# Two weight subtractions moved from VectorE to GpSimd, and the last row tile scaled by two engines

## The chip, the core and the metric

The kernel runs on one core of a Trainium2 chip. The metric is the device time of one execution in microseconds; lower is better. The core's engines run side by side, each through its own queue in order, and wait for one another through semaphores: TensorE (PE, with PEld for its weight loads), VectorE (DVE), ScalarE (ACT), GpSimd (POOL) and SyncE (SP, which issues most DMAs). GpSimd computes too, and it issues the DMAs that gather and scatter rows by a list.

## What is computed

Three layers follow each other, cut here to what matters:

```python
# 1: attention over keys and values averaged in groups of 8
scores = scale * q @ k_pooled.T;  attn = softmax(scores);  x = attn @ v_pooled   # -> 4608 x 512
# 2: a dense layer, 512 -> 2048 -> 512, with ELU between
x = elu(x @ w_in) @ w_out
# 3: a mixture of 8 experts, 512 -> 1024 -> 512, one expert per token
logits = x @ w_gate;  expert_idx = argmax(logits, axis=1);  gate_w = softmax(logits)[.., expert_idx]
for e in range(E):
    xe = x[expert_idx == e]
    h = np.maximum(xe @ w1[e], 0.0)
    out[expert_idx == e] = gate_w[expert_idx == e, None] * (h @ w2[e])
```

Everything is float32. The kernel multiplies at reduced precision with a correction: an operand is split into a high part (a cast to fp32r) and a low part (the operand minus its high part), and high x high, low x high and high x low are added up in PSUM.

## The kernel before

The change lies in the last stage, the experts. Tokens are sorted into lists by expert, and the lists are cut into tiles that the code runs one after the other: eight D tiles of 512 tokens, one S tile of 256 tokens (`S0`) and three T tiles of 128 tokens; three small U tiles of at most 32 tokens run beside others. The order of the tiles is D0 to D6, T0, D7, T1, S0, T2. So `main[-1]` is T2, a tile of one row group of 128 tokens, and S0 is the second to last.

A tile has four **units** (`i` = 0 to 3), each with 256 columns of the expert's hidden layer. For each unit:

- `m_load` issues two loads of 512 KB on SP, the first layer's weights (`w1st`, in T tiles `t1`) and the second layer's (`w2st`);
- `m_split` makes their high parts (`m1h`, `m2h`) with a ScalarE cast and their low parts (`m1l`, `m2l`) with a subtraction, by `split` at lines 129 to 131. Its parameter `eng` names the engine of the second layer's subtraction; without it that is VectorE. T tiles split the second layer alone;
- `m_g1` multiplies the tokens (`zh`, `zl`) with the first layer into `mh`; `m_act` applies the ReLU on ScalarE (`hh`) and makes the low part on VectorE (`hl`); `m_g2` multiplies `hh` and `hl` with the second layer and adds up into `my`, in the order `hh` x `m2h`, `hh` x `m2l`, `hl` x `m2h`.

`m_out` scales a finished tile's rows by the gate into `o`, ScalarE for even row groups and VectorE for odd ones, and `scatter` writes them to the output with an indirect DMA issued by GpSimd.

The order on each engine is the order in which the code is written, under a manual schedule. The function `mix(n)` writes step n: the first layer of unit n, the second layer of unit n - 1, the activations, the output of a tile that ended. Then `ahead(n)` lets loads and splits run ahead of their use, as far as a pool of 32 equal pieces of memory (`w_tile`) and reach limits allow. Freed pieces go to a queue and are given out again in turn, so a new tile can lie in the space of an older one; whoever writes it first waits for the older one's last reader. Around the change this gives: in the step where T1 starts, S0's units 1 and 2 are split; in the next, S0's unit 3; between them the low part of T1's own activations (`hlT`) is made on VectorE.

Of the kernel before, what the change touches and what calls it, by code (L numbers as in the profile page):

```python
# [20 lines left out]
B, H, S, D = 8, 8, 576, 64  # L21
POOLW = 8
SP = S // POOLW
DM = H * D
# [74 lines left out]
def fused_kernel(ctx: ExitStack, tc: tile.TileContext, q, k, v, w_in, w_out, w_gate, w1, w2, cst, out):  # L99
    nc = tc.nc  # L100
# [28 lines left out]
    def split(hi, lo, src, eng=None):  # L129
        nc.scalar.copy(hi, src)  # L130
        (eng or nc.vector).tensor_sub(lo, src, hi)
# [13 lines left out]
    def ring(pool, shape, dtype, tag, bufs, name):  # L145
        k = turns[tag] = (turns.get(tag, -1) + 1) % bufs
        return pool.tile(shape, dtype, tag=f"{tag}{k}", bufs=1, name=name)
# [19 lines left out]
    def w_tile(shape, dtype, name):  # L167
        slot_w[name] = k = free_w.pop(0)
        return wpool.tile(shape, dtype, tag=f"W{k}", bufs=1, name=name)

    def w_free(*names):
        for name in names:
            free_w.append(slot_w.pop(name))
# [904 lines left out]
    rows, sidxs, zs, wts, raws2, acts, yps, gates = {}, {}, {}, {}, {}, {}, {}, {}  # L1078
# [147 lines left out]
    def m_split(it, i, eng=None):  # L1226
        kind, s = it
        st, st2 = raws2.pop((it, i))
        if kind != "T":
            first = [w_tile([P, KC, 2 * P], F32R, f"m1{x}{kind}{s}_{i}") for x in "hl"]  # L1230
            split(*first, st)
        else:
            first = [st]
        second = [w_tile([P, 2, DM], F32R, f"m2{x}{kind}{s}_{i}") for x in "hl"]
        split(*second, st2, eng)
        wts[it].append((first, second))
        for name in (f"w1st{kind}{s}_{i}", f"w2st{kind}{s}_{i}"):
            if name in slot_w:
                w_free(name)
            if name in slot_s:  # L1240
                free_s.append(slot_s.pop(name))
# [65 lines left out]
    def m_out(it, i):  # L1307
        kind, s = it
        nu = TILES[kind]
        if i == 3:  # L1310
            for u in range(nu):
                o = ring(pools[1], [P, DM], F32, "o", 4, f"o{kind}{s}_{u}")
                gate = gates[it][:, u:u + 1]
                if u % 2 == 0:
                    nc.scalar.mul(o, yps[it][u], gate)
                else:
                    nc.vector.tensor_scalar_mul(o, yps[it][u], gate)
                scatter(out[:, :], o, sidxs[it][0][:, u:u + 1], NTOK)

    def scatter(dst, src, idx, n):  # L1320
        put = nc.gpsimd.indirect_dma_start(
            out=dst,
            out_offset=bass.IndirectOffsetOnAxis(ap=idx, axis=0),
            in_=src,
            in_offset=None,
            bounds_check=n - 1,
            oob_is_err=False,
        )
        tc.declare_no_dep(put.ins, group="out", reason="each token's row is written once")
        tc.add_to_no_dep_group("out", put.ins)  # L1330
# [53 lines left out]
    main = [("D", s) for s in range(KD)]  # L1384
# [45 lines left out]
    def ahead(n):  # L1430
        done = False
        while not done:
            done = True
            for what, reach, src in (("load", LOAD_REACH, units), ("split", SPLIT_REACH, split_units)):
                x = todo[what]
                if x == len(src):
                    continue
                need, it, i = src[x]
                if what == "split" and (need, it, i) not in units[:todo["load"]]:
                    continue  # L1440
                if need - when[n] > reach:
                    continue
                slots = SLOTS[it[0]][what == "split"]
                raw = STAGES[it[0]]
                if what == "load":
                    slots += max(0, raw - len(free_s))
                    if need - when[n] > 6 and raw > len(free_s) and len(free_w) < 12:
                        continue
                if slots > len(free_w):
                    continue  # L1450
                if what == "load":
                    m_load(it, i)
                else:
                    m_split(it, i)
                todo[what] += 1
                done = False

# [12 lines left out]
    for k in range(TURN_FROM, len(main)):  # L1470
        it, far = main[k], main[k - 1][0] == "T"
# [47 lines left out]
    def mix(n):  # L1519
# [11 lines left out]
        if n:  # L1531
            m_out(main[k0], i0)
# [3 lines left out]
        if n in casts_first:  # L1536
            for _, it2, half in todo_now:
                m_room(it2, half)
            ahead(n)
        elif k in side and i == 3:  # L1540
            u_out(side[k])
# [31 lines left out]
    with tc.manual_schedule(engines=ENGINES):  # L1573
        ahead(0)
        for n in range(8):
            mix(n)
        lpool["p"] = pools[1]
        for n in range(8, len(seq)):
            mix(n)
            if n == len(seq) - 6:  # L1580
                nc.gpsimd.drain()
        k0, i0 = seq[-1]
        m_g2(main[k0], i0)
        m_out(main[k0], i0)
# [85 lines left out]
```

## Time and profile before

| | |
|---|---|
| median of 3 runs | 1354.22 us (1353.72 to 1355.11) |
| the profiled execution | 1353.46 us, of it the span 1351.6 us |
| PE busy | 1336.7 us, 99% of the span |
| DVE busy | 1024.4 us, 76% |
| ACT busy | 798.8 us, 59% |
| POOL busy | 205.0 us, 15% |
| mean granted TensorE clock | 0.996 |
| S0's unit 1 split to the last scatter | about 1297 to 1347 us of the span |

The span is what the profiler saw of one execution; 1.9 us lie around it. A busy share is an average over the whole span. What a change at one place is worth is read from the engines' timelines at that place, by which wait ends last. In a row of a timeline a bracket gives the idle time of the engine just before the instruction and what ended it; a row without one followed at once.

### The profile page before, as it was taken

What the parts mean: (1) busy time and instruction counts of PE and PEld (TensorE: products, weight loads), DVE (VectorE), ACT (ScalarE), POOL (GpSimd) and SP (SyncE); (2) the same over time, 40 slices, a digit from 0 to 9 for tenths busy, and PEclk for the clock granted to TensorE, in tenths of its full rate; (3) what the DMA queues carried; (4) which work ended last, traced back from release to release, by engine and by line L of the source; (5) the groups of instructions that cost most, each with busy time, mean ns of one, the idle gap of its engine ahead of it and who ended that gap; (6) DMA issues with size and microseconds to landing.
All of it is one profiled execution on the core that took longest, in us unless ns stands there. A gap on an engine that the chain in (4) does not pass through costs nothing.

```text
span 1351.6 us, 23742 instructions
## 1 busy us (share of the span) xinstructions
PE 1336.7 (99%) x8398; PEld 1152.7 (85%) x8398; DVE 1024.4 (76%) x2479; ACT 798.8 (59%) x1949; POOL 205.0 (15%) x208
## 2 busy tenths in 40 slices
PE   9999999999999999999999999999999999999998
PEld 5799888888888889898988888988888888788787
DVE  7899888998888879797878787886646766646471
ACT  6777766676667676666666665562333444536261
POOL 0011011101211211111210000020213131212020
PEclk9999999999999999999999999999999999999999
DMA  9257443647354463555472432465576357768470
GB/s 349 71 175 213 126 100 83 84 78 80 74 80 70 83 69 63 86 66 82 73 94 48 64 40 47 90 161 117 164 119 186 125 179 257 267 200 299 156 275 23
DMA packets 109145, 169.43 MB, mean 125 GB/s; under 512 B 15509, under 2 KB 53015, under 8 KB 109016
## 3 DMA queue, kind: packets, MB, share of 16 engines
q1 hardware_dynamic: 91528, 135.45, 40.7%
q0 software_dynamic: 17488, 32.37, 12.5%
q8 instruction: 68, 1.11, 0.4%
q14 instruction: 61, 0.50, 0.2%
HBM read 146.35 MB, written 21.88 MB: 124 GB/s over the span
## 4 chain that ended last, share of the span: by engine, by line
PE 80%; DVE 8%; issue 5%; ACT 4%; DMA 2%; POOL 0%; SPq 0%; POOLq 0%; DVEq 0%; ACTq 0%
PE h L507 25%; PE y L549 25%; PE mhD L1261 12%; PE myD L1298 12%; PE pv L480 3%; PE sp L411 1%; DVE dec L228 1%; DVE dec L232 1%; DMA w2stD<-in_moe_w_dram 1%; DVE junk L600 1%; ACT gh L531 1%; ACT dec L221 1%; PE vsum L346 1%; DVE dec L226 1%; DVE g L524 1%
## 5 line engine op out<-in xcount | busy, mean ns | idle before, releaser
L549 PE MATMUL y<-woh,gh 128*128 128x512 f32 x576 | 229.8, 399 | 0.9 <-DVE yr L563 0.5
L549 PE MATMUL y<-woh,gl 128*128 128x512 f32 x576 | 226.4, 393 | 0.0
L549 PE MATMUL y<-wol,gh 128*128 128x512 f32 x576 | 226.2, 393 | 0.0
L600 DVE SCALAR_TENSOR_TENSOR junk<-yr,wgb 128x512 bf16<-128x512 f32 x264 | 180.9, 685 | 4.7 <-ACT yr L565 1.2
L531 ACT CAST gh<-g 128x384 fp32r<-128x384 f32 x192 | 98.5, 513 | 131.0 <-DVE g L525 111.9
L507 PE MATMUL h<-xh,wih 128*128 128x384 f32 x768 | 167.8, 340 | 2.3 <-ACT xh L493 1.5
L507 PE MATMUL h<-xl,wih 128*128 128x384 f32 x768 | 165.8, 337 | 0.0
L507 PE MATMUL h<-xh,wil 128*128 128x384 f32 x768 | 165.6, 337 | 0.0
L524 DVE SCALAR_TENSOR_TENSOR g<-g,th 128x384 f32<-128x384 f32 x192 | 106.3, 554 | 73.3 <-ACT th L519 72.7
L507 PEld LDWEIGHTS h<-xh,wih 128*128 128x128 f32 x768 | 138.3, 188 | 19.4 <-DVE g L525 2.1
L517 ACT ACTIVATE th<-h 128x384 f32<-128x384 f32 x192 | 94.1, 490 | 84.8 <-PE h L507 84.1
L1275 ACT ACTIVATE hhD<-mhD 128x512 fp32r<-128x512 f32 x64 | 38.3, 598 | 179.0 <-PE myD L1298 168.8
L507 PEld LDWEIGHTS h<-xh,wil 128*128 128x128 f32 x768 | 137.1, 188 | 0.0
L507 PEld LDWEIGHTS h<-xl,wih 128*128 128x128 f32 x768 | 136.9, 188 | 0.2
L1276 DVE SCALAR_TENSOR_TENSOR hlD<-mhD,hhD 128x512 fp32r<-128x512 f32 x64 | 44.2, 690 | 122.5 <-ACT hhD L1275 122.5
L549 PEld LDWEIGHTS y<-woh,gl 128*128 128x128 f32 x576 | 108.2, 188 | 23.6
L549 PEld LDWEIGHTS y<-woh,gh 128*128 128x128 f32 x576 | 108.1, 188 | 21.4 <-issue 1.0
L549 PEld LDWEIGHTS y<-wol,gh 128*128 128x128 f32 x576 | 108.2, 188 | 16.7
L532 DVE TENSOR_TENSOR gl<-g,gh 128x384 fp32r<-128x384 f32 x192 | 106.9, 557 | 19.9 <-ACT gh L531 17.0
L525 DVE TENSOR_TENSOR g<-g,h 128x384 f32<-128x384 f32 x192 | 106.3, 554 | 6.6
L519 ACT ACTIVATE th<-th 128x384 f32<-128x384 f32 x192 | 100.9, 525 | 6.1
L518 ACT ACTIVATE g<-th 128x384 f32<-128x384 f32 x192 | 100.9, 525 | 6.1
(287 smaller groups left out, 2387.2 us busy)
## 6 DMA issues: line engine op xcount, KB each, us to landing
wgb<-in_moe_w_gate_dram SPq DMA_DIRECT2D x96, 256.0 KB
w1stD<-in_moe_w_dram SPq DMA_DIRECT2D x32, 512.0 KB
w2stD<-in_moe_w_dram SPq DMA_DIRECT2D x32, 512.0 KB
qT<-in_q_dram SPq DMA_DIRECT2D x36, 256.0 KB
ybuf<-yr SPq DMA_DIRECT2D x33, 256.5 KB
raw<-in_moe_w_in_dram SPq DMA_DIRECT2D x16, 512.0 KB
raw<-in_moe_w_out_dram SPq DMA_DIRECT2D x15, 512.0 KB
t1U<-in_moe_w_dram SPq DMA_DIRECT2D x12, 512.0 KB
```

Source lines behind the costliest of these rows:

```text
L507: mark["g1"] = nc.tensor.matmul(ps, wi[i][a][:, c, o:o + P], bb[blk][:, c, :], start=n == 0, stop=n == 3 * KC - 1).ins
L517: nc.scalar.activation(th, hps[blk, f], AF.Relu, scale=-1.0)
L518: nc.scalar.activation(g, th, AF.Exp, scale=-1.0)
L519: nc.scalar.activation(th, th, AF.Tanh, scale=-0.5)
L524: nc.vector.scalar_tensor_tensor(g, g, 1.0, th, op0=ALU.add, op1=ALU.mult)
L525: nc.vector.tensor_max(g, g, hps.pop((blk, f)))
L531: nc.scalar.copy(gh, g)
L532: nc.vector.tensor_sub(gl, g, gh)
L549: nc.tensor.matmul(ys[blk][j], a[:, js], wo[i][bb][:, o, :], start=n == 0 and f in FIRST[blk], stop=n == 2 and f in LAST[blk],)
L600: nc.vector.scalar_tensor_tensor(junk, yrows[blk][j][:, :DM], 1.0, pes[blk, e], op0=ALU.mult, op1=ALU.mult, accum_out=lgs[blk][:, j, e:e + 1])
L1261: mark["g1"] = nc.tensor.matmul(ps[:, x], a[:, c, o * P:(o + 1) * P], y[:, c], start=k == 0, stop=k == len(terms) - 1).ins
L1298: nc.tensor.matmul(yps[it][u], a[:, us], second[w][:, o], start=i == 0 and o == 0 and n == 0, stop=i == 3 and o == 1 and n == 2,)
```

## The change

Two edits. In `ahead`, `m_split` gets GpSimd as its engine for units 1 and 2 of S tiles; of these tiles only S0 runs, so two subtractions of 128x1024 change the engine. In `m_out`, the last tile's row group is cut into two halves of 256 columns, the first scaled by ScalarE and the second by VectorE; the scatter behind them is the same.

```diff
             for u in range(nu):
                 o = ring(pools[1], [P, DM], F32, "o", 4, f"o{kind}{s}_{u}")
                 gate = gates[it][:, u:u + 1]
-                if u % 2 == 0:
+                if it == main[-1]:
+                    half = DM // 2
+                    nc.scalar.mul(o[:, :half], yps[it][u][:, :half], gate)
+                    nc.vector.tensor_scalar_mul(o[:, half:], yps[it][u][:, half:], gate)
+                elif u % 2 == 0:
                     nc.scalar.mul(o, yps[it][u], gate)
...
                 if what == "load":
                     m_load(it, i)
                 else:
-                    m_split(it, i)
+                    m_split(it, i, nc.gpsimd if it[0] == "S" and i in (1, 2) else None)
```

The order shows what this does to the queues. Numbers in names are tile and unit: `m2lS0_1` is the low part of the second layer's weights of S0's unit 1, `oD7_3` the fourth row group of D7's output. In brackets stand the semaphores for which a row waits, by the engine or the DMA queue that counts them. GpSimd's queue at the end of D7, before:

```order
L1321 DMA out_0_dram<-oD7_0_14501,oidxD7_12701 4608x512 [waits DMAHW5_49,DMASW0_49,Activation_49]
L1321 DMA out_0_dram<-oD7_1_14506,oidxD7_12701 4608x512 [waits DMASW1_49,DVE_49]
L1321 DMA out_0_dram<-oD7_2_14511,oidxD7_12701 4608x512 [waits DMASW2_49,Activation_49]
L1321 DMA out_0_dram<-oD7_3_14516,oidxD7_12701 4608x512 [waits DMASW3_49,DVE_49]
L1321 DMA out_0_dram<-oT1_0_14675,oidxT1_13152 4608x512 [waits DMAHW2_49,DMASW4_49,Activation_49]
```

and now:

```order
L1325 DMA out_0_dram<-oD7_0_14501,oidxD7_12701 4608x512 [waits DMAHW5_49,DMASW0_49,Activation_49]
L1325 DMA out_0_dram<-oD7_1_14506,oidxD7_12701 4608x512 [waits DMASW1_49,DVE_49]
L1325 DMA out_0_dram<-oD7_2_14511,oidxD7_12701 4608x512 [waits DMASW2_49,Activation_49]
L1325 DMA out_0_dram<-oD7_3_14516,oidxD7_12701 4608x512 [waits DMASW3_49,DVE_49]
L131 ISA
L131 TENSOR_TENSOR m2lS0_1_14530<-w2stS0_1_14421,m2hS0_1_14529 128x1024 [waits DMAHW6_49,DMAHW2_49,Activation_49]
L131 TENSOR_TENSOR m2lS0_2_14551<-w2stS0_2_14429,m2hS0_2_14550 128x1024 [waits DMAHW1_49,DMAHW0_49,DMAHW5_49,PE_49,Activation_49]
L1325 DMA out_0_dram<-oT1_0_14675,oidxT1_13152 4608x512 [waits DMASW4_49,Activation_49]
```

The two subtractions stand between D7's last scatter and T1's, and an `ISA` row came in ahead of them; the built program names this instruction a reload of a library, with index 0. VectorE's queue at the same place, before:

```order
L131 TENSOR_TENSOR m1lS0_1_14526<-w1stS0_1_14419,m1hS0_1_14525 128x1024 [waits DMAHW5_49,Activation_49]
L131 TENSOR_TENSOR m2lS0_1_14530<-w2stS0_1_14421,m2hS0_1_14529 128x1024 [waits DMAHW6_49,Activation_49]
L131 TENSOR_TENSOR m1lS0_2_14547<-w1stS0_2_14427,m1hS0_2_14546 128x1024 [waits DMAHW7_49,Activation_49]
L131 TENSOR_TENSOR m2lS0_2_14551<-w2stS0_2_14429,m2hS0_2_14550 128x1024 [waits DMAHW0_49,Activation_49]
L1276 SCALAR_TENSOR_TENSOR hlT1_1_0_14575<-mhT1_1_0_14558,hhT1_1_0_14574 128x256 [waits DVE_49,Activation_49]
L131 TENSOR_TENSOR m1lS0_3_14579<-w1stS0_3_14521,m1hS0_3_14578 128x1024 [waits DMAHW1_49,Activation_49]
L131 TENSOR_TENSOR m2lS0_3_14583<-w2stS0_3_14523,m2hS0_3_14582 128x1024 [waits DMAHW2_49,DVE_49,Activation_49]
L1175 TENSOR_TENSOR zlS0_14600<-zmS0_0_14418,zhS0_14599 128x4x256 [waits Activation_49]
L1276 SCALAR_TENSOR_TENSOR hlT1_2_0_14610<-mhT1_2_0_14590,hhT1_2_0_14609 128x256 [waits Activation_49]
```

and now:

```order
L131 TENSOR_TENSOR m1lS0_1_14526<-w1stS0_1_14419,m1hS0_1_14525 128x1024 [waits DMAHW5_49,Activation_49]
L131 TENSOR_TENSOR m1lS0_2_14547<-w1stS0_2_14427,m1hS0_2_14546 128x1024 [waits DMAHW7_49,Activation_49]
L1276 SCALAR_TENSOR_TENSOR hlT1_1_0_14575<-mhT1_1_0_14558,hhT1_1_0_14574 128x256 [waits DVE_49,Activation_49]
L131 TENSOR_TENSOR m1lS0_3_14579<-w1stS0_3_14521,m1hS0_3_14578 128x1024 [waits DMAHW1_49,Activation_49]
L131 TENSOR_TENSOR m2lS0_3_14583<-w2stS0_3_14523,m2hS0_3_14582 128x1024 [waits DMAHW2_49,DMAHW6_49,Activation_49,Pool_49]
L1175 TENSOR_TENSOR zlS0_14600<-zmS0_0_14418,zhS0_14599 128x4x256 [waits DVE_49,Activation_49]
L1276 SCALAR_TENSOR_TENSOR hlT1_2_0_14610<-mhT1_2_0_14590,hhT1_2_0_14609 128x256 [waits DVE_49,Activation_49]
```

`m2lS0_1` and `m2lS0_2` are gone here, and `m2lS0_3`, the low part of unit 3, now waits for GpSimd's counter (`Pool_49`, at its value after the first subtraction): it is written to the piece of memory that `w2stS0_1` has given back. In the same way SP's load `t1T2_2` waits for GpSimd's second subtraction in place of VectorE. The end of VectorE's queue, before:

```order
L1276 SCALAR_TENSOR_TENSOR hlT2_0_0_14849<-mhT2_0_0_14827,hhT2_0_0_14848 128x256 [waits Activation_49]
L1317 TENSOR_SCALAR oS0_1_14857<-myS0_1_14710,gateS0_14293 128x512 [waits DMASW3_49,DMASW2_49,PE_49]
L1276 SCALAR_TENSOR_TENSOR hlT2_1_0_14879<-mhT2_1_0_14862,hhT2_1_0_14878 128x256 [waits Activation_49]
L1276 SCALAR_TENSOR_TENSOR hlT2_2_0_14898<-mhT2_2_0_14882,hhT2_2_0_14897 128x256 [waits Activation_49]
L1276 SCALAR_TENSOR_TENSOR hlT2_3_0_14917<-mhT2_3_0_14901,hhT2_3_0_14916 128x256 [waits Activation_49]
L1610 TENSOR_LOAD tot_11679 [waits DVE_49]
```

and now:

```order
L1276 SCALAR_TENSOR_TENSOR hlT2_1_0_14879<-mhT2_1_0_14862,hhT2_1_0_14878 128x256 [waits Activation_49]
L1276 SCALAR_TENSOR_TENSOR hlT2_2_0_14898<-mhT2_2_0_14882,hhT2_2_0_14897 128x256 [waits Activation_49]
L1276 SCALAR_TENSOR_TENSOR hlT2_3_0_14917<-mhT2_3_0_14901,hhT2_3_0_14916 128x256 [waits Activation_49]
L1317 TENSOR_SCALAR oT2_0_14926<-myT2_0_14871,gateT2_14760 128x256 [waits DMASW3_49,Activation_49]
L1614 TENSOR_LOAD tot_11679 [waits DVE_49]
```

VectorE's half of T2's rows (`oT2`) is new, and it waits for ScalarE's counter at its value after ScalarE's half; the scatter of `oT2` on GpSimd waits for VectorE's counter where it waited for ScalarE's.

## Rows read from the trace of the kernel before

**Rows 1.** The page, part 1: busy us (share of the span) xinstructions

```profile
PE 1336.7 (99%) x8398; PEld 1152.7 (85%) x8398; DVE 1024.4 (76%) x2479; ACT 798.8 (59%) x1949; POOL 205.0 (15%) x208
```

**Rows 2.** Timeline of PE, 1302 to 1309 us: start, us, what [idle before <-releaser]

```profile
1303.18 0.50 PE L1298 MATMUL myT<-m2hT,hlT 128*128 128x512 f32 x1 [0.62 <-DVE hlT L1276]
...
1306.91 0.50 PE L1298 MATMUL myT<-m2hT,hlT 128*128 128x512 f32 x1 [0.29 <-DVE hlT L1276]
```

**Rows 3.** Timeline of DVE, 1301 to 1307 us

```profile
1301.57 1.22 DVE L131 TENSOR_TENSOR m2lS<-w2stS,m2hS 128x1024 fp32r<-128x1024 f32 x1
1302.70 0.42 DVE L1276 SCALAR_TENSOR_TENSOR hlT<-mhT,hhT 128x256 fp32r<-128x256 f32 x1
...
1304.17 1.22 DVE L131 TENSOR_TENSOR m2lS<-w2stS,m2hS 128x1024 fp32r<-128x1024 f32 x1
1305.31 1.22 DVE L1175 TENSOR_TENSOR zlS<-zmS,zhS 128x1024 fp32r<-128x1024 f32 x1
1306.44 0.75 DVE L1276 SCALAR_TENSOR_TENSOR hlT<-mhT,hhT 128x256 fp32r<-128x256 f32 x2
```

**Rows 4.** Timeline of POOL, 1295 to 1352 us

```profile
1298.61 1.63 POOL L1321 DMA_INDIRECT out_dram<-oD,oidxD  x1 [0.30 <-issue]
1300.55 1.96 POOL L1321 DMA_INDIRECT out_dram<-oD,oidxD  x1 [0.30 <-issue]
1302.81 0.98 POOL L1321 DMA_INDIRECT out_dram<-oD,oidxD  x1 [0.31 <-DVE m2lS L131]
1313.37 0.98 POOL L1321 DMA_INDIRECT out_dram<-oT,oidxT  x1 [9.57 <-ACT oT L1315]
```

**Rows 5.** Waits of POOL, whole span: us in total, times, longest us

```profile
POOL tab L675 <- DMA tab<-toki,rpi: 190.8, 23, 14.1
...
POOL kT L311 <- DMA kT<-in_k_dram: 147.5, 35, 17.9
```

**Rows 6.** Timelines of SP, 1301 to 1307 us, and ACT, 1305 to 1346 us

```profile
1302.82 0.37 SPq L1211 DMA_DIRECT2D t1T<-in_moe_w_dram  x1
...
1315.77 1.99 ACT L130 CAST m2hT<-w2stT 128x1024 fp32r<-128x1024 f32 x2
```

**Rows 7.** Groups by line of POOL: xcount | busy us, mean ns | idle before

```profile
L260 POOL CAST tri<-tri_st 128x128 bf16<-128x128 f32 x1 | 0.4, 425 | 32.0 <-DMA tri_st<-in_const_dram 32.0
L252 POOL MEMSET fill<- 128x292 int32 x1 | 0.3, 341 | 0.3 <-POOLq L1654 0.3
L441 POOL MEMSET s_wide<- 128x64 f32 x1 | 0.2, 152 | 34.5 <-PE aTp L463 34.5
```

**Rows 8.** Windows: us, busy PE, PEld, DVE, ACT, POOL, PEclk, DMA share, GB/s

```profile
1348.00:1348.50 0.50, 0.00 (x0) 0.00 (x0) 0.00 (x0) 0.00 (x0) 0.00 (x0) 1.00 0.35 115
1348.50:1349.00 0.50, 0.00 (x0) 0.00 (x0) 0.00 (x0) 0.00 (x0) 0.00 (x0) 0.51 0.07 25
```

**Rows 9.** Timeline of PE, 32 to 43 us, and two windows there

```profile
32.80 1.65 PE L507 MATMUL h<-xh,wih 128*128 128x384 f32 x4
...
36.94 1.03 PE L463 MATMUL aTp<-ident,s 64*72 64x64 f32 x16
...
40.25 0.97 PE L507 MATMUL h<-xh,wih 128*128 128x384 f32 x4
...
42.47 1.02 PE L346 MATMUL vsum<-natv,sums 128*72 128x512 f32 x2
...
37.00:37.50 0.50, 0.50 (x13) 0.50 (x14) 0.00 (x0) 0.40 (x1) 0.00 (x0) 0.50 1.02 377
40.00:42.00 2.00, 2.00 (x16) 1.83 (x13) 1.91 (x4) 2.00 (x16) 0.00 (x0) 1.00 0.35 137
```

**Rows 10.** Timelines of ACT and DVE, 1339 to 1346 us

```profile
1342.31 0.38 ACT L1275 ACTIVATE hhT<-mhT 128x256 fp32r<-128x256 f32 x1 [2.78 <-PE mhT L1261]
1345.05 0.69 ACT L1315 ACTIVATE oT<-myT,gateT 128x512 f32<-128x512 f32 x1 [2.35 <-PE myT L1298]
...
1342.73 0.42 DVE L1276 SCALAR_TENSOR_TENSOR hlT<-mhT,hhT 128x256 fp32r<-128x256 f32 x1 [2.73 <-ACT hhT L1275]
```

## The prediction

> **What bounds the kernel now.** I read the page's busy shares first: TensorE works 99% of the span [rows 1], so an edit on another engine counts only where it alters what TensorE waits for. Then the timeline of TensorE around the edit, from 1290 us to the end. It waits twice there, 0.62 us ahead of 1303.18 and 0.29 us ahead of 1306.91, both times for `hlT`, the low part of tile T1's activations that VectorE makes [rows 2]. After 1306.91 it has no idle time again up to the last matmul, so what delays that one matmul delays the end. VectorE's timeline says why `hlT` is late: ahead of the second one stand `m2lS` of unit 3 at 1304.17 and `zlS` at 1305.31, back to back [rows 3]. From the start of that `m2lS` to TensorE's restart it is 1306.91 - 1304.17 = 2.74 us. Last GpSimd's timeline: it issues the scatters of tile D7 one after the other, and the fourth ends at 1302.81 + 0.98 = 1303.79 [rows 4].
>
> **Part 1: two subtractions leave VectorE.** `m2lS` of units 1 and 2 take about 1.13 us each there (the second from 1301.57 to the next instruction's start at 1302.70) [rows 3]. `hlT` of T1's unit 1, behind them, comes earlier, and the wait of 0.62 us goes. By itself that is worth nothing more than a place further along: TensorE then reaches the next `hlT` sooner and waits for that one.
>
> **Part 2: they enter GpSimd's queue, and VectorE waits for it.** In the order, they stand behind D7's four scatters, so the first can't begin before 1303.79 plus the usual gap between two GpSimd instructions, 0.30 us [rows 4]: 1304.09. In the order too, VectorE's `m2lS` of unit 3 now waits for GpSimd: its tile lies in the space that `w2stS` of unit 1 gives back, which the first GpSimd subtraction still reads. Queued behind the waiting instruction on VectorE are `zlS` and the `hlT` for which TensorE waits. So a wait that was not there stands in front of the one chain that TensorE follows, and its length is the reload plus the subtraction:
>
> - The order has one more instruction on GpSimd, `ISA`, right ahead of the first subtraction; the built program names it a reload of the code library. The kernel before has none after its start, so no row prices it. Below: 0, if the code is there already. Above: it must fetch, and the nearest rows are GpSimd's waits for its own transfers: 147.5 us in 35 waits (4.2 us each) for loads from DRAM, 190.8 us in 23 (8.3 us) for writes of the table, the longest 17.9 us [rows 5]; with 0.98 us to issue, 5.2 and 9.3 us. I take 6.5, nearer to the loads, because a fetch of code is a load. The rings were nearly full here before, but the four loads that SP would issue from 1302.82 on [rows 6] wait for GpSimd now, which frees them.
> - The Trainium skill (GPSIMD Engine Reference, 2.1 Instruction dispatch) says that the first call to freshly loaded code costs about 6 us with no instruction visible in the profile. No run here shows it yet. With 6 in place of 6.5 the sum would be half a microsecond lower.
> - The subtraction itself: below, VectorE's 1.22 us [rows 3]. Above, GpSimd's slowest float cast, 0.425 us for 128 columns, is 3.3 ns a column, for 1024 columns 3.4 us [rows 7]. Between: the two memsets give (341 - 152) / (292 - 64) = 0.83 ns a column for one stream [rows 7]; two reads and a write one after the other make 3 x 0.83 x 1024 = 2.5 us. I take 2.5, since the cast's 0.425 us holds a fixed part that a long instruction pays once.
>
> The first subtraction ends at 1304.09 + 6.5 + 2.5 = 1313.1. `m2lS` of unit 3 starts then instead of at 1304.17: **8.9 us** later, and `zlS`, `hlT` and TensorE follow at their old distance of 2.74 us, so TensorE resumes at 1315.8.
>
> **Part 3: the clock.** TensorE then stands still from about 1306.0 (1306.91 less both waits) to 1315.8. The trace has one idle stretch as long, after the last matmul (the scaling that it releases starts at 1345.05 [rows 10]): the granted clock is 1.00, or 2.4 GHz, in the half microsecond before 1348.5 and 0.51, or 1.2 GHz, in the one after it [rows 8], some 3.5 us after the work stopped. So it will be low when TensorE resumes. What that costs is seen near the start of the kernel: twelve matmuls of line 507 take from 32.80 to the next work at 36.94, 4.14 us, and the clock is still 0.50 just after; the next twelve take from 40.25 to 42.47, 2.22 us, at 1.00 [rows 9]. That is 1.9 us lost in twelve matmuls, with the low stretch going on past them. I take **2.3 us**, bounds 0 (no fall) and 3.
>
> **Part 4: the rest of what moves.** TensorE reads the two GpSimd results only in tile S0's own second layer, for units 1 and 2, after the rest of T1 and S0's first unit; with an end of the second subtraction at 1313.1 + 2.5 = 1315.6, before TensorE has even resumed, that costs nothing. SP's load `t1T` of T2's unit 2 waits for GpSimd's second subtraction and holds the three loads behind it: issued at 1302.82, first used by ScalarE at 1315.77 [rows 6], 13 us. The issue slips to 1315.6, the use to about 1327, so 11 us stay for loads that are alone on the rings. Behind the subtractions on GpSimd stands the scatter of `oT` of T1, at 1313.37 because it waits for ScalarE [rows 4]; it slips with TensorE and costs nothing.
>
> **Part 5: the last rows.** The order makes VectorE's half wait for ScalarE's half, and the scatter for VectorE: the halves run one after the other. A whole takes ScalarE 0.69 us at 1345.05; 128x256 takes ScalarE 0.38 and VectorE 0.42 us, which starts 0.04 us after ScalarE's ends (1342.31 + 0.38, 1342.73) [rows 10]. With ScalarE's half at 0.43 (a little above, as the whole is above its like), 0.43 + 0.04 + 0.42 = 0.89 against 0.69: **0.2 us** longer. If they ran side by side it would be 0.25 shorter.
>
> **Sum.** 8.9 + 2.3 + 0.2 = 11.4 us. On the profiled execution, 1353.46 us with a span of 1351.6, that is 1364.9; on the median of 1354.22, 0.8 above it, **1365.6**.
>
> **Rivals.**
>
> - *Shared access.* VectorE's `m2lS` of unit 3 and GpSimd's second subtraction become free at the same moment. If the second one holds VectorE off until its end, 2.5 us are added: 1368.1. For it: GpSimd needs no signal to go on. Against: in these rows a VectorE subtraction beside a GpSimd scatter takes its usual 1.22 us [rows 3, 4]; but a scatter is no arithmetic. A rule on this is in the Trainium skill (SBUF — State Buffer, Who interferes with whom): a VectorE instruction with two SBUF inputs and a GpSimd instruction that reads SBUF exclude each other for the whole instruction. No run here shows it yet; by it this rival is the outcome.
> - *The reload is free.* Then the delay is 2.5 - 0.1 = 2.4 us, TensorE stands still for 2.4 + 0.9 = 3.3 us, short of the 3.5 after which the clock fell, and with 0.2 for the rows the time is 1356.8, at the edge of no change. For it: GpSimd runs casts and memsets without one [rows 7].
> - *The reload waits in the rings* like the table's writes, 9.3 us: 1368.4; like the longest, 17.9 us: 1377.0.
> - *Not slower.* The second and third scatter of D7 take 1.63 and 1.96 us instead of 0.98 [rows 4]. If VectorE's subtractions beside them are the cause and these are gone, GpSimd is free 1.6 us sooner, at 1302.46; with no price for the reload and VectorE's 1.22 us the first subtraction ends at 1303.7. It decides at 1304.17: below that VectorE doesn't wait, and TensorE's 0.62 and 0.29 us go, less 0.2 for the rows: 0.7 us gained, 1353.5. It needs three things at once, the fourth scatter's own 0.98 among what stays.
>
> **How the numbers follow.** Forecast 0.44, shared access 0.25, longer reload 0.15, free reload 0.13, not slower 0.03. The range of 1357 to 1372 leaves out the last, half of the free reload and the upper part of the longer one. About 0.2%, 2.7 us, is what a measurement of this kernel tells from no change: all of the first three and half of the fourth lie above it, so slower 0.89, same 0.10; a gain of 2.7 us has no wait of that size to come from, faster 0.01.
>
> **What would show it.** Right: GpSimd's first subtraction begins 5 to 8 us after D7's fourth scatter ends; VectorE's `m2lS` of unit 3 is released by GpSimd; one idle stretch of 8 to 12 us on TensorE ends with `hlT`; the granted clock is 0.5 for some microseconds after it; the last scatter follows a VectorE instruction. Wrong: a gap of less than 1 us there (free reload), `m2lS` starting at the end of the second subtraction (shared access), or TensorE idle at the uses of `m2lS` of units 1 or 2.

## The result and the profile after

The changed kernel takes 1361.53 us (median of 6 runs, 1360.26 to 1362.79), the kernel before 1354.52 in the same session: 7.0 us slower. The ratio on record is 1.0061, 95% interval 1.0048 to 1.0073, which is 6.5 to 9.9 us; it isn't the quotient of these two medians (1.0052). The forecast was 1365.6 with a range of 1357 to 1372: right in sign and place, 4.1 us too high.

One execution differs from the next by a few microseconds, from work far ahead of the change. So beside the medians I compare two stretches inside the profiled executions. They begin where GpSimd starts the scatter of the U tile's rows (`uo`), which stands ahead of everything that the change moves, and they end where TensorE resumes with `hlT` of T1's unit 2, and where GpSimd starts the last scatter. Before, the second one is 1346.01 - 1295.99 = 50.02 us; after, 1352.82 - 1296.29 = 56.53, thus 6.51 more.

The page's busy times say little: TensorE is still busy for 98% of the span, GpSimd is busy for 2.8 us more and VectorE for as much as before, although it makes two subtractions less [rows 1].

```profile
PE 1335.8 (98%) x8397; PEld 1152.3 (85%) x8398; DVE 1024.3 (75%) x2478; ACT 798.5 (59%) x1949; POOL 207.8 (15%) x210
```

GpSimd's, VectorE's and TensorE's timelines of the changed kernel, at the place of the first edit (compare [rows 2 to 4]):

```profile
1296.29 1.01 POOL L1325 DMA_INDIRECT out_dram<-uo,oidxU  x1 [23.59 <-ACT hhT L1275]
...
1300.84 1.58 POOL L1325 DMA_INDIRECT out_dram<-oD,oidxD  x1 [0.30 <-PE myT L1298]
1302.73 1.86 POOL L1325 DMA_INDIRECT out_dram<-oD,oidxD  x1 [0.30 <-issue]
1304.68 4.68 POOL L131 TENSOR_TENSOR m2lS<-w2stS,m2hS 128x1024 fp32r<-128x1024 f32 x2
...
1300.35 1.23 DVE L131 TENSOR_TENSOR m1lS<-w1stS,m1hS 128x1024 fp32r<-128x1024 f32 x1 [0.67 <-ACT m1hS L130]
1301.57 0.42 DVE L1276 SCALAR_TENSOR_TENSOR hlT<-mhT,hhT 128x256 fp32r<-128x256 f32 x1
1302.51 1.23 DVE L131 TENSOR_TENSOR m1lS<-w1stS,m1hS 128x1024 fp32r<-128x1024 f32 x1 [0.51 <-ACT m1hS L130]
1307.10 3.35 DVE L131 TENSOR_TENSOR m2lS<-w2stS,m2hS 128x1024 fp32r<-128x1024 f32 x1 [3.36 <-POOL m2lS L131]
1310.38 1.21 DVE L1175 TENSOR_TENSOR zlS<-zmS,zhS 128x1024 fp32r<-128x1024 f32 x1
1311.51 0.74 DVE L1276 SCALAR_TENSOR_TENSOR hlT<-mhT,hhT 128x256 fp32r<-128x256 f32 x2
...
1311.98 0.80 PE L1298 MATMUL myT<-m2hT,hlT 128*128 128x512 f32 x1 [5.96 <-DVE hlT L1276]
```

Four things are to be seen. GpSimd's first subtraction starts 0.09 us after the fourth scatter ends (1302.73 + 1.86 = 1304.59): no reload of 6.5 us. A subtraction takes GpSimd 4.68 / 2 = 2.34 us. VectorE's `m2lS` of unit 3 is released by GpSimd's first subtraction at 1307.10, and then it takes 3.35 us where it took 1.22 [rows 3]; it ends 1.09 us after GpSimd's second subtraction does (1309.36). And TensorE has one wait of 5.96 us where it had two of 0.62 and 0.29 [rows 2].

Windows of the same kernel (us, busy time of PE, PEld, DVE, ACT and POOL, granted clock, DMA share, GB/s):

```profile
1307.00:1308.00 1.00, 0.00 (x0) 0.00 (x0) 0.90 (x1) 0.00 (x0) 1.00 (x2) 1.00 0.07 27
1308.00:1308.50 0.50, 0.00 (x0) 0.00 (x0) 0.50 (x1) 0.00 (x0) 0.50 (x1) 0.89 0.00 0
1308.50:1315.00 6.50, 3.02 (x10) 2.66 (x11) 4.88 (x5) 0.00 (x0) 0.86 (x1) 0.50 0.61 202
1315.00:1315.50 0.50, 0.50 (x5) 0.50 (x5) 0.00 (x0) 0.00 (x0) 0.00 (x0) 0.79 1.08 379
```

TensorE stopped at 1306.02. The granted clock fell from 1.00 (2.4 GHz) to 0.50 (1.2 GHz) in the half microsecond behind 1308.0, 2.0 to 2.5 us after the stop, and was back within half a microsecond behind 1315.0, so TensorE worked its first 3 us behind the wait at half speed.

The last rows, ScalarE, VectorE and GpSimd:

```profile
1351.55 0.48 ACT L1316 ACTIVATE oT<-myT,gateT 128x256 f32<-128x256 f32 x1 [2.35 <-PE myT L1298]
...
1352.06 0.48 DVE L1317 TENSOR_SCALAR oT<-myT,gateT 128x256 f32<-128x256 f32 x1 [2.40 <-ACT oT L1316]
...
1352.82 0.97 POOL L1325 DMA_INDIRECT out_dram<-oT,oidxT  x1 [9.57 <-DVE oT L1317]
```

The halves run one behind the other, 1.27 us from ScalarE's start to the scatter.

The 6.51 us are made of three parts. TensorE resumes 1311.98 - 1296.29 = 15.69 us behind `uo` instead of 1306.91 - 1295.99 = 10.92: 4.77. From there to ScalarE's scaling of the last rows it is 39.57 us instead of 1345.05 - 1306.91 = 38.14 [rows 2, 10]: 1.43. From that scaling to the scatter it is 1.27 instead of 0.96: 0.31.

Rows of the kernel before that [rows 3, 4] don't show, the first and last scatter and three of VectorE's subtractions:

```profile
1295.99 1.01 POOL L1321 DMA_INDIRECT out_dram<-uo,oidxU  x1 [23.60 <-ACT hhT L1275]
...
1346.01 0.98 POOL L1321 DMA_INDIRECT out_dram<-oT,oidxT  x1 [9.26 <-ACT oT L1315]
...
1298.16 1.23 DVE L131 TENSOR_TENSOR m1lS<-w1stS,m1hS 128x1024 fp32r<-128x1024 f32 x1 [0.22 <-ACT m1hS L130]
1299.30 1.22 DVE L131 TENSOR_TENSOR m2lS<-w2stS,m2hS 128x1024 fp32r<-128x1024 f32 x1
1300.43 1.22 DVE L131 TENSOR_TENSOR m1lS<-w1stS,m1hS 128x1024 fp32r<-128x1024 f32 x1
```

### The profile page after: what moved, and what is told of

Its sections match the earlier page's. It is cut to its first block, busy times and chain, and to the rows that moved or that the text cites. A ratio compares the mean times of both kernels' runs of the same rounds, so it can differ in the third digit from the quotient of the medians.

```text
span 1358.2 us, 23749 instructions
## 1 busy us (share of the span) xinstructions
PE 1335.8 (98%) x8397; PEld 1152.3 (85%) x8398; DVE 1024.3 (75%) x2478; ACT 798.5 (59%) x1949; POOL 207.8 (15%) x210
## 4 chain that ended last, share of the span: by engine, by line
PE 80%; DVE 9%; ACT 5%; DMA 3%; issue 3%; POOL 0%; SPq 0%; POOLq 0%; ACTq 0%; DVEq 0%
PE h L507 24%; PE y L549 23%; PE mhD L1261 12%; PE myD L1298 12%; PE pv L480 2%; DVE junk L600 1%; PE sp L411 1%; DMA wgb<-in_moe_w_gate_dram 1%; DVE dec L228 1%; DVE dec L232 1%; DMA w2stD<-in_moe_w_dram 1%; ACT gh L531 1%; PE mhS L1261 1%; PE myS L1298 1%; DVE g L524 1%
```

## Theories

**Held:** a VectorE subtraction with both operands in the on-chip memory (SBUF) and a GpSimd instruction that reads there exclude each other for their whole length. That makes 3.35 us of 1.22, and explains the scatters as well. The loss is then GpSimd's place in the queue and 2.34 us, plus the holding, plus the low clock, plus the last rows. **Wait alone:** only the wait for the piece of memory that `w2stS` of unit 1 gives back counts, and the 3.35 us have another cause, the weights that arrive at that time for one. A third question is whether the library load, free in the trace, **hides in the fourth scatter**, which took 1.86 us instead of 0.98.

All measurements in one table. Times are from the profiled executions in us: A from `uo`'s scatter to TensorE's resumption, B from there to ScalarE's scaling of the last rows, C from `uo`'s scatter to the last scatter. The ratio is to the kernel before, with its 95% interval.

| kernel | A | B | C | ratio |
|---|---|---|---|---|
| before | 10.92 | 38.14 | 50.02 | 1 |
| changed | 15.69 | 39.57 | 56.53 | 1.0061 (1.0048 to 1.0073) |
| last rows alone | 10.92 | 38.13 | 50.32 | 1.0004 (0.9994 to 1.0014) |
| subtractions alone | 15.68 | 39.86 | 56.50 | 1.0058 (1.0037 to 1.0080) |
| unit 1 alone on GpSimd | 12.89 | 39.63 | 53.79 | 1.0025 (1.0015 to 1.0036) |
| another piece of memory | 12.27 | 39.42 | 52.96 | 1.0024 (1.0014 to 1.0035) |
| zeros in place of the second | 13.56 | 39.63 | 54.46 | 1.0032 (1.0022 to 1.0042) |
| a copy in place of the second | 14.37 | 39.51 | 55.15 | one run, 1360.36 us |
| units 1 to 3 on GpSimd | 16.84 | 40.31 | 58.11 | 1.0061 (1.0049 to 1.0074) |
| the same, library loaded early | 16.77 | 39.89 | 57.62 | 1.0051 (1.0034 to 1.0068) |
| changed, library loaded early | 15.61 | 40.42 | 57.30 | 1.0061 (1.0041 to 1.0081) |
| changed, TensorE kept busy | 15.71 | 38.14 | 55.11 | 1.0037 (1.0024 to 1.0050) |
| before, subtractions later | 9.73 | 38.12 | 48.82 | 0.9985 (0.9976 to 0.9993) |

## Experiment 1: each edit alone

```diff
-                    m_split(it, i, nc.gpsimd if it[0] == "S" and i in (1, 2) else None)
+                    m_split(it, i)
```

> Only the last rows are changed; the two subtractions stay on VectorE. All theories agree: the two halves run one behind the other, so the scatter of the last rows starts about 0.3 us later than before and the time is 1354.8 us (before 1354.5). TensorE keeps the two waits of 0.62 and 0.29 us of the kernel before, and GpSimd's four scatters ahead of the tile take 7.8 us in sum as before. If the last rows carried more of the loss than the trace of the changed kernel shows, the time would be above 1356.

Measured: 1353.88 us where before took 1353.63, and C is 0.30 us longer. TensorE, with its waits of 0.62 and 0.31 us, is where it was.

```diff
-                if it == main[-1]:
-                    half = DM // 2
-                    nc.scalar.mul(o[:, :half], yps[it][u][:, :half], gate)
-                    nc.vector.tensor_scalar_mul(o[:, half:], yps[it][u][:, half:], gate)
-                elif u % 2 == 0:
+                if u % 2 == 0:
```

> Only the two subtractions go to GpSimd; the last rows are scaled as before. All theories agree on the time: the changed kernel's 1361.5 us less 0.3, thus 1361.2. The run is here to show whether the parts of the loss (a start of GpSimd's first subtraction right behind its fourth scatter, 3.35 us for VectorE's low part of unit 3, 5 us of wait on TensorE) come back without the other edit, and whether the fourth scatter takes 1.86 us again instead of 0.98: if it does here and not where GpSimd makes no subtraction, the load of GpSimd's library may hide in it.

Measured: 1361.41 us. GpSimd, VectorE and TensorE show the same durations as with both edits: scatters of 1.63, 1.58 and 1.86 us, then

```profile
1302.29 4.69 POOL L131 TENSOR_TENSOR m2lS<-w2stS,m2hS 128x1024 fp32r<-128x1024 f32 x2
...
1304.72 3.35 DVE L131 TENSOR_TENSOR m2lS<-w2stS,m2hS 128x1024 fp32r<-128x1024 f32 x1 [3.37 <-POOL m2lS L131]
...
1309.60 0.80 PE L1298 MATMUL myT<-m2hT,hlT 128*128 128x512 f32 x1 [5.96 <-DVE hlT L1276]
```

The edits don't touch each other: the subtractions carry the loss, and the last rows 0.3 us, too little for their own interval to tell from nothing. The two C of this experiment add up to 0.27 us more than both edits cost together; B of the subtractions alone, in which the low clock lies, is 0.29 longer.

## Experiment 2: GpSimd's second subtraction, and the wait, taken away one at a time

Only unit 1 goes to GpSimd, so that the wait stays and nothing runs on GpSimd behind it:

```diff
-                    m_split(it, i, nc.gpsimd if it[0] == "S" and i in (1, 2) else None)
+                    m_split(it, i, nc.gpsimd if it[0] == "S" and i in (1,) else None)
```

> GpSimd makes the low part of unit 1 alone; unit 2's is VectorE's again, ahead of the wait. Theory held (GpSimd's second subtraction holds VectorE's subtraction back while it reads): the low part of unit 3 takes 1.22 us again instead of 3.35, TensorE resumes about 2.1 us earlier than in the changed kernel (at 1309.8 instead of 1312.0), and the time is 2.1 to 3.0 us less, 1358.5 to 1359.4. Theory of a slow VectorE instruction from another cause (the wait alone counts, and 3.35 us comes from weights arriving at the same time): it takes about 3.3 us again and the time stays within 0.4 us of 1361.5.

GpSimd and VectorE:

```profile
1303.38 0.98 POOL L1325 DMA_INDIRECT out_dram<-oD,oidxD  x1 [0.30 <-DVE m2lS L131]
1304.45 2.60 POOL L131 TENSOR_TENSOR m2lS<-w2stS,m2hS 128x1024 fp32r<-128x1024 f32 x1
...
1303.61 1.22 DVE L131 TENSOR_TENSOR m1lS<-w1stS,m1hS 128x1024 fp32r<-128x1024 f32 x1
1307.08 1.23 DVE L131 TENSOR_TENSOR m2lS<-w2stS,m2hS 128x1024 fp32r<-128x1024 f32 x1 [2.26 <-POOL m2lS L131]
```

`m2lS` of unit 3 takes 1.23 us again, though it is released in the same way: the second subtraction was what stretched it, and the wait-alone theory's 3.3 us are refuted. C is 2.74 us shorter than with both, within the 2.1 to 3.0 expected. The two ratios differ by more, 0.36% or 4.9 us, but the near ends of their intervals only by 0.12% or 1.6 us, so 2.7 lies within. The time itself, 1356.94, is below the 1358.5 to 1359.4 that I gave. Nor is all of the 2.74 the holding: `m2lS` is 2.12 us shorter, and GpSimd's first subtraction ends 10.11 us behind `uo` instead of 10.73, because the fourth scatter takes 0.98 us here and not 1.86. Here GpSimd is the one that is held: it starts at 1304.45 beside VectorE's subtraction of 1303.61, which ends at 1304.8, and takes 2.60 us instead of 2.34.

Next the wait goes and the second subtraction stays: the low part of unit 3 gets another free piece.

```diff
-        second = [w_tile([P, 2, DM], F32R, f"m2{x}{kind}{s}_{i}") for x in "hl"]
+        second = [w_tile([P, 2, DM], F32R, f"m2h{kind}{s}_{i}")]
+        if (kind, s, i) == ("S", 0, 3):
+            free_w.insert(0, free_w.pop(3))
+        second.append(w_tile([P, 2, DM], F32R, f"m2l{kind}{s}_{i}"))
```

> The low part of unit 3 gets another free piece of memory, so that it no longer waits for GpSimd's first subtraction; nothing else is changed. Theory held: the low part of unit 3 runs at 1304.2 in 1.22 us, and the next VectorE subtraction (the low part of the 256-token tile's rows) is held until GpSimd's first (1307.0) or second subtraction (1309.4) ends, so TensorE resumes between 1308.5 and 1311 and the time is 1356.5 to 1360.5. Theory that the wait for the piece is all of the loss: TensorE resumes at 1306.9 as before, and only the 0.3 us of the last rows are left, 1354.8.

```profile
1302.72 5.72 POOL L131 TENSOR_TENSOR m2lS<-w2stS,m2hS 128x1024 fp32r<-128x1024 f32 x2
...
1301.69 1.22 DVE L131 TENSOR_TENSOR m2lS<-w2stS,m2hS 128x1024 fp32r<-128x1024 f32 x1
1302.83 3.39 DVE L1175 TENSOR_TENSOR zlS<-zmS,zhS 128x1024 fp32r<-128x1024 f32 x1
1306.14 0.74 DVE L1279 SCALAR_TENSOR_TENSOR hlT<-mhT,hhT 128x256 fp32r<-128x256 f32 x2
1306.80 2.71 DVE L131 TENSOR_TENSOR m2lT<-w2stT,m2hT 128x1024 fp32r<-128x1024 f32 x1
```

No wait for GpSimd is left, and `zlS`, issued 0.11 us behind GpSimd's first subtraction, takes 3.39 us: 2.34 from GpSimd's start end at 1305.06, and 1.1 more end at 1306.1, where `hlT` starts. Then GpSimd's second subtraction, which had to let `zlS` through, holds `m2lT`. In between, `hlT`, which has one operand in PSUM, takes 0.74 us as ever (0.75 in [rows 3]) while that second subtraction runs. TensorE resumes 1.35 us later than before, not at the same place as the wait-alone theory has it. The time, 1356.05, is just under the lower end that I gave.

## Experiment 3: what GpSimd has to do to hold VectorE

In place of the second subtraction, zeros are written, so that unit 2's low part is missing from the result; in the other kernel the line with the zeros reads `eng.tensor_copy(second[1], st2)`.

```diff
-        split(*second, st2, eng)
+        if eng and i == 2:
+            nc.scalar.copy(second[0], st2)
+            eng.memset(second[1].bitcast(F32), 0.0)
+        else:
+            split(*second, st2, eng)
```

> GpSimd writes zeros instead of its second subtraction (unit 2's low part is left out of the result): an instruction that reads nothing, in the place of one that reads two tiles. Theory that what holds VectorE's two-operand subtraction is GpSimd's use of the memory by an instruction of any kind: the low part of unit 3, which waits for the first subtraction as in the changed kernel, takes longer than 1.22 us, by as long as the write lasts (1.2 to 3 us). Theory that only GpSimd's instructions with two operands in that memory hold it: 1.22 us beside the write, and TensorE resumes 2.1 us earlier than in the changed kernel, at 1309.8.

> GpSimd copies unit 2's staged weights in place of its second subtraction (unit 2's low part is left out of the result): one operand instead of two. With zeros written there, VectorE's low part of unit 3 took 1.23 us. Theory that any GpSimd instruction that reads the memory holds VectorE's two-operand subtraction: it takes about 1.1 us more than what is left of the copy when it is issued, over 1.5 us. Theory that only two operands on both sides meet: 1.23 us beside the copy.

With zeros:

```profile
1305.76 0.97 POOL L1237 MEMSET m2lS<- 128x1024 f32 x1
...
1305.86 1.23 DVE L131 TENSOR_TENSOR m2lS<-w2stS,m2hS 128x1024 fp32r<-128x1024 f32 x1 [3.36 <-POOL m2lS L131]
```

With a copy:

```profile
1307.39 1.07 POOL L1237 CAST m2lS<-w2stS 128x1024 fp32r<-128x1024 f32 x1
1307.51 2.04 DVE L131 TENSOR_TENSOR m2lS<-w2stS,m2hS 128x1024 fp32r<-128x1024 f32 x1 [3.37 <-POOL m2lS L131]
```

Beside the write VectorE's subtraction takes 1.23 us, and A is 2.13 us shorter than in the changed kernel. Beside the copy it takes 2.04: it ends 1.09 us after the copy (1308.46). So it takes a GpSimd instruction that reads, and one operand is enough. The Trainium skill (SBUF — State Buffer, Who interferes with whom) says this of a VectorE instruction with two SBUF inputs and a GpSimd instruction that reads SBUF, and excepts one that only writes; 2.04 and 1.23 agree.

## Experiment 4: the library load

A small GpSimd subtraction at the kernel's start brings the `ISA` row there; in the order it is gone from the place ahead of the large ones.

```diff
         nc.gpsimd.tensor_copy(toki, tri_st[:, P:])
+        nc.gpsimd.tensor_sub(tri_st[:, :P], tri_st[:, :P], tri_st[:, :P])
```

> The changed kernel with one small GpSimd subtraction of 128x128 at the kernel's start (on a tile whose values have been read), so that the load of GpSimd's library stands there and no longer between the fourth scatter and the first large subtraction. Theory that the load is free: the fourth scatter takes 1.86 us (0.88 us to the end of VectorE's running subtraction, then 0.98) as in the changed kernel, the first large subtraction starts 0.09 us behind it or less, TensorE resumes 15.7 us behind the start of the first of the scatters, and the time stays at 1361.5. Theory that the load hides in the scatter or the gap: the fourth scatter takes 0.98 us, all that follows is 0.9 us earlier (14.8 us), and the time is 0.9 us less.

```profile
1302.74 1.85 POOL L1326 DMA_INDIRECT out_dram<-oD,oidxD  x1 [0.30 <-issue]
1304.59 4.70 POOL L131 TENSOR_TENSOR m2lS<-w2stS,m2hS 128x1024 fp32r<-128x1024 f32 x2
```

The scatter takes 1.85 us without a load behind it, and the subtraction starts 0.00 us behind it instead of 0.09. The load costs 0.09 us and hides nowhere. Whether it had anything to fetch, or the library of index 0 was there already, no run tells. What stretches the scatter is VectorE's `m1lS` of 1302.51, which holds it to 1303.6; 0.98 us follow. The same sum fits the long scatters of the kernel before: `m1lS` at 1298.16 and at 1300.43 give way to the next instruction at 1299.30 and 1301.57, and 0.98 behind that is where the scatters of 1.63 and 1.96 us end, 1300.24 and 1302.51 [rows 4]. The scatter of 1302.81 stands beside `hlT`, one operand in PSUM, and takes 0.98. The exclusion is one-sided, though: `m2lS` of 1299.30 runs beside the last 0.9 us of the first of these scatters and takes its usual 1.22. A scatter waits for VectorE's subtraction and doesn't hold it.

## Experiment 5: all three units on GpSimd

With unit 3's low part on GpSimd too, no VectorE instruction waits for GpSimd ahead of `hlT`. This could have been the better form of the change. The edit is to the kernel before, so the last rows are scaled as there.

```diff
-                    m_split(it, i)
+                    m_split(it, i, nc.gpsimd if it[0] == "S" and i in (1, 2, 3) else None)
```

> GpSimd makes unit 3's low part too, and the last rows are scaled as before. VectorE's queue then has no wait for GpSimd ahead of the tile's rows. Theory held: if VectorE starts the low part of the tile's rows before GpSimd's first subtraction (1304.7 in the changed kernel), GpSimd waits for it, TensorE waits at neither place, and the time is 0.9 us less than before, 1352.7; if VectorE comes later, that row is held for one GpSimd subtraction, TensorE resumes near 1308.5 to 1309, and the time is 1.6 to 3.5 us more than before, 1355.2 to 1357.1. Theory that the wait for the piece of memory is all of the loss: 1352.7 to 1353.6 in either order.

```profile
1304.65 6.97 POOL L131 TENSOR_TENSOR m2lS<-w2stS,m2hS 128x1024 fp32r<-128x1024 f32 x3
...
1304.37 8.34 DVE L1175 TENSOR_TENSOR zlS<-zmS,zhS 128x1024 fp32r<-128x1024 f32 x1 [0.67 <-DVE m1lS L131]
```

Neither of my cases: `zlS` was held for all three subtractions, 8.34 us, although its row begins 0.28 us ahead of the first. It ends 1.09 us after the third (1311.62). GpSimd's subtractions stand back to back and none of them lets it in. In experiment 2 they stood back to back too, and there the same row, begun 0.11 us behind the first, got in ahead of the second. The time is 1361.81, as bad as the change itself. Perhaps the library load between scatter and subtraction took the access first; so once more with the load at the kernel's start:

> GpSimd makes the low parts of units 1 to 3, with the library loaded at the kernel's start. With the load in its old place VectorE's low part of the tile's rows began 0.28 us ahead of GpSimd's first subtraction and was held for all three, 8.34 us. Theory that the load takes the shared access ahead of the subtraction: that row now runs in 1.22 us, GpSimd's first subtraction waits for it, TensorE has no wait there, and the time is 0.9 us less than before (1352.7 where before is 1353.6). Theory that the subtraction's own start is what matters, and that the recorded start of VectorE's instruction is up to 0.3 us ahead of its reads: 8.3 us again, and the time 1361.8.

```profile
1305.72 7.00 POOL L131 TENSOR_TENSOR m2lS<-w2stS,m2hS 128x1024 fp32r<-128x1024 f32 x3
...
1305.55 8.26 DVE L1176 TENSOR_TENSOR zlS<-zmS,zhS 128x1024 fp32r<-128x1024 f32 x1 [0.67 <-ACT zhS L1175]
```

8.26 us again: it wasn't the load. Why a row that begins 0.17 or 0.28 us earlier loses, and why it got in after one subtraction in experiment 2 and after none here, stays open. The last tenths of a scatter run beside its start; but a scatter alone doesn't hold such a row (in experiment 7 `zlS` begins at 1302.29 beside a scatter that ends at 1302.48, and takes 1.22 us).

## Experiment 6: the clock

26 matmuls on a tile of ones fill TensorE's wait.

```diff
+                    if (it, i, o, n) == (("T", 1), 2, 0, 2):
+                        ps = bank_z([P, 4, P], "busy")
+                        for _ in range(26):
+                            nc.tensor.matmul(
+                                ps, ones, ones.unsqueeze(1).to_broadcast([P, 4, P]), start=True, stop=True
+                            )
                     nc.tensor.matmul(
                         yps[it][u],
```

> The changed kernel with 26 matmuls of 128x512 on a tile of ones put into TensorE's wait (a result that nobody reads), so that TensorE works through the 6 us in which it waits for VectorE. At 0.21 us each they fill 5.5 us and end before VectorE's low part comes (1312.0), so they delay nothing by themselves. Theory that the fall of the clock costs 1.4 us behind the wait: the granted clock stays at 1.00 through 1315, the distance from TensorE's resumption to the last rows' ScalarE half falls from 39.57 to 38.1 us as in the kernel before, and the time is 1.4 us less, 1360.1. Theory that the low clock is covered by other waits there: the distance stays near 39.6 us and the time at 1361.5.

TensorE's timeline, and two windows:

```profile
1302.24 5.79 PE L1301 MATMUL busy<-ones 128*128 128x512 bf16 x26
1308.38 0.50 PE L1304 MATMUL myT<-m2hT,hlT 128*128 128x512 f32 x1 [0.35 <-DVE hlT L1276]
...
1308.00:1312.00 4.00, 3.65 (x27) 3.45 (x27) 1.78 (x3) 0.00 (x0) 0.00 (x0) 1.00 0.97 307
1312.00:1315.00 3.00, 3.00 (x22) 2.74 (x21) 0.69 (x1) 1.73 (x3) 0.16 (x1) 1.00 0.49 183
```

A is 15.71 as in the changed kernel, the clock stays at 1.00, and B is 38.14, to the hundredth that of the kernel before. So the low clock is all of the 1.43 us behind TensorE's resumption, and nothing else that the change moved costs anything there. C falls by 1.42. The median, 1357.42, lies further below the changed kernel's than the 1.4 us that I gave. The ratio falls by more, 0.24% or 3.3 us, with 0.13% or 1.8 us of uncertainty to either side of each of the two, so the size is taken from the trace.

## Experiment 7: the kernel before, its subtractions later

The same three low parts stay on VectorE, but behind `zlS` and the `hlT` of unit 2; they are used only in S0's own second layer.

```diff
+        if (kind, s) == ("S", 0) and i:
+            nc.scalar.copy(second[0], st2)
+            late.append((second, st2, f"w2st{kind}{s}_{i}"))
...
+            return
         split(*second, st2, eng)
...
+    def m_late():
+        second, st2, name = late.pop(0)
+        nc.vector.tensor_sub(second[1], st2, second[0])
...
+        while late and it == ("T", 1) and i >= 2:
+            m_late()
```

> The kernel before with VectorE's low parts of units 1 to 3 moved behind the tile's rows and behind the low part that TensorE waits for; GpSimd makes none. Both waits of TensorE in this stretch (0.62 and 0.29 us) should go, and nothing on GpSimd can hold VectorE: 0.9 us less than before, 1352.7 of 1353.6. If the three subtractions, 3.4 us in a row, now stand ahead of a low part that TensorE needs soon (that of unit 3 of the 128-token tile), a new wait of up to 0.5 us takes the place, and the time stays within 0.5 us of before.

VectorE, and TensorE's matmul that waited before:

```profile
1302.29 1.22 DVE L1175 TENSOR_TENSOR zlS<-zmS,zhS 128x1024 fp32r<-128x1024 f32 x1 [0.67 <-ACT zhS L1174]
1303.43 0.42 DVE L1296 SCALAR_TENSOR_TENSOR hlT<-mhT,hhT 128x256 fp32r<-128x256 f32 x1
1303.77 3.49 DVE L1257 TENSOR_TENSOR m2lS<-w2stS,m2hS 128x1024 fp32r<-128x1024 f32 x3
1307.17 0.42 DVE L1296 SCALAR_TENSOR_TENSOR hlT<-mhT,hhT 128x256 fp32r<-128x256 f32 x1
...
1303.91 0.50 PE L1318 MATMUL myT<-m2hT,hlT 128*128 128x512 f32 x1
```

TensorE has no wait left in this stretch. A is 1.19 us shorter, of which the two waits make 0.91, C 1.20, and the time is 1351.15 where before took 1353.29: 0.15% less, the interval 0.07% to 0.24%. It beats both kernels, by taking VectorE's subtractions out of `hlT`'s way and not off VectorE.

## Why the prediction came out as it did

- **The place and the chain: right.** TensorE, `hlT`, `zlS`, `m2lS` of unit 3, GpSimd's first subtraction: that chain ends TensorE's one wait. The wait was 5.96 us, under the 8 to 12 that it named.
- **Part 1: right.** Without the two subtractions the 0.62 us wait goes, and TensorE only stops earlier, at 1306.02 (forecast about 1306.0).
- **Part 2, the reload: the step that failed.** 6.5 us forecast, 0.09 measured (experiment 4). The step priced it by GpSimd's waits for its own data transfers [rows 5], rows of another kind; the lower bound of 0 was all but the value. The 6 us that the Trainium skill (GPSIMD Engine Reference, 2.1 Instruction dispatch) gives for a first call to freshly loaded code don't show at the kernel's start either, where the small subtraction, in its first call, begins at 34.63, behind a cast that ends at 34.58.
- **Part 2, the subtraction: right in size, and by luck.** 2.5 forecast, 2.34 measured. The working, three streams of 0.83 ns a column one after the other, would give a copy two of them, 1.7 us; a copy took 1.07, hardly more than the 0.97 of the zeros (experiment 3). Its start, apart from the reload, was 0.20 us later than forecast: the fourth scatter was held and ended 0.50 later, and the gap of 0.30, which is that ahead of a scatter, didn't come.
- **The rival of shared access: it came true**, as a mechanism, at a chance of 0.25: 3.35 - 1.22 = 2.13 us, where it had 2.5. It came together with the free reload, which had stood as a rival of its own; the forecast had each alone. The argument against it misread the rows: it looked only at whether VectorE is longer beside a scatter. It isn't; the scatters were [rows 4], and each of them by what was left of VectorE's subtraction. The rival "not slower" even asked whether VectorE's subtractions stretch the scatters, and took no conclusion from it for the subtractions.
- **Part 3: right, mis-sized.** 2.3 forecast (0 to 3), 1.43 measured, 1.28 to 2.28 over the runs with a wait (B in the table). That the clock falls only some 3.5 us after the work stops was read from one place; here it fell 2.0 to 2.5 us after. The free-reload rival took no loss for a stop of 3.3 us on that ground, and a shorter stop was enough: with unit 1 alone (experiment 2) TensorE stood for 2.62 us, the clock was still 1.00 when it resumed at 1309.83, it was 0.50 by 1311.0, and 1.49 us were lost (B):

```profile
1309.50:1310.50 1.00, 0.67 (x3) 0.58 (x4) 1.00 (x3) 0.00 (x0) 0.00 (x0) 1.00 1.06 392
1311.00:1314.00 3.00, 3.00 (x16) 3.00 (x15) 0.24 (x1) 0.00 (x0) 0.00 (x0) 0.50 0.63 236
```

- **Part 4: right**, B of 38.14 in experiment 6.
- **Part 5: right in mechanism, a little short.** 0.2 forecast, 0.31 measured: the halves take 0.48 us each where I had 0.43 and 0.42.

In one line, from the forecast's delay on `hlT`: 8.92 - 6.41 (reload) + 0.20 (start) - 0.16 (subtraction) + 0.08 (gap to the release) + 2.13 (held) = 4.76, the 4.77 of the trace; with 1.43 and 0.31 it is 6.5 instead of 11.4. That the forecast is 4.1 us off and not more is in part luck, since the two large errors have opposite signs. The range, 15 us wide, didn't need it: with zeros in place of the second subtraction, thus without the holding, C grows by 4.44 us, and 1354.22 + 4.44 = 1358.7 still lies within. The chances that the forecast adds up to 0.89 for slower make 0.44 + 0.25 + 0.15 + 0.065 = 0.905.

## What to carry to other kernels

Before moving a subtraction from VectorE to GpSimd, look on both sides for pairs that overlap: a GpSimd row that is longer by just the rest of a VectorE row has waited for it, which is a reason to price the opposite case too. It doesn't show that case: the scatters here held nothing, the subtractions did. A run of GpSimd subtractions held VectorE to its end in experiment 5 and let it in after the first in experiment 2, so count on the longer of the two. What VectorE's work cost here was decided by its place in the queue ahead of the instruction for which TensorE waits (experiment 7), so first try to put it behind that instruction on the same engine. Price an instruction that no row shows by rows of its own kind or leave its range open down to nothing.

## What the runs showed of the hardware

- GpSimd takes 2.34 us for a subtraction of 128x1024 (VectorE 1.22), 1.07 for a copy and 0.97 for zeros of that size.
- An indirect scatter on GpSimd waits for a VectorE subtraction that runs with both operands in the on-chip memory, then takes its 0.98 us (1.58 to 1.96 in all); the other way round it holds nothing (1.22 us beside it).
- The reload of GpSimd's library 0 between two instructions took 0.09 us.
- The clock's fall isn't the same from one execution to the next. With the library loaded early TensorE stops at 1306.02 too (1311.91 - 5.89), but the granted clock is still 1.00 up to 1310.0:

```profile
1309.00:1310.00 1.00, 0.00 (x0) 0.00 (x0) 1.00 (x1) 0.00 (x0) 0.29 (x1) 1.00 0.00 0
1310.00:1310.50 0.50, 0.00 (x0) 0.00 (x0) 0.50 (x2) 0.00 (x0) 0.00 (x0) 0.71 0.29 37
1310.50:1317.00 6.50, 5.09 (x20) 4.71 (x21) 2.81 (x4) 0.00 (x0) 0.00 (x0) 0.50 0.89 300
```

More of the low stretch then falls on work, 5.09 us of it instead of 3.02, and B is 40.42 instead of 39.57.
